# Token sums converted one step per second product, and three more PSUM banks in the first batch, in a fused sparse-attention and expert kernel

## The chip, the cores and the metric

The kernel runs on one core of a Trainium2 chip. The core has five engines with a queue each: PE (TensorE, matrix products, with its weight loads shown apart as PEld), DVE (VectorE), ACT (ScalarE), POOL (GpSimd) and SP (SyncE, which here only starts DMAs). An engine takes its instructions in the order of its queue, and one that waits holds up those behind it. The matrix results lie in PSUM, eight banks per partition. The metric is device time in microseconds, the median of three runs; the profile is one more execution with its own time.

## The reference

Two stages follow each other. The attention works on 4 batches, 8 heads, 768 tokens and 64 columns a head; a query block of 32 tokens sees its neighbours, the first and the last block, and three sampled blocks. The experts then take the attention's output `x` (3072 tokens by 512):

```
x = attention(q, k, v, sampled_blocks)         # 4 batches x 768 tokens, 512 columns
p = domain_probs / (sum(domain_probs) + 1e-9)
for e in range(4):
    h = max(x @ w1[e], 0)                      # 512 -> 1024
    out += p[:, e] * (h @ w2[e])               # 1024 -> 512
```

## The kernel before, in words

The first batch's attention runs alone, up to about 95 us. Then the experts of batch b run while the attention of batch b+1 is spread through them by `drive`. All five engines keep the order in which the program writes the instructions; no scheduler moves them.

The experts of a batch are cut into 8 chunks `c` (two for each expert, 512 hidden columns each). Inputs are kept as a high and a low part, so each product takes three matmuls for one. A step `first` makes one half product with `w1`: 6 matmuls of 128x384 (L537) into a PSUM bank. A step `second` makes 3 matmuls of 128x512 with `w2` (L595) into one of three banks `po`, and after four hidden tiles DVE adds the bank into `oacc` (L610).

Chunks 1 to 7 take seven products of sums of token blocks and of weight blocks for what would be eight plain ones; `ORDER` lists them. Chunk 0, the plain chunk, takes eight plain products of two steps each (`FIRST`, 16 steps), from the token blocks as they are: the operands `xo` 1, 2, 7 and 3. The first six products of chunk 0 follow each other on PE without a step `second` between them; this text calls them P0 to P5. They write the banks `v`, `w`, `v`, `w`, `v`, `w` (L551, `"vw"[i % 2]`, one buffer each). After the second step of a product, `finish` (L541) has ACT write the high part `hh` (L544) and then DVE the low part `hl` (L545); both read the bank, so the bank comes free when `hl` is written. `hl0` to `hl5` and `hh0` to `hh5` are those of P0 to P5.

The tokens' operands are made by the generator `conversion(b)` in 14 pieces, each one call of `convert`: a cast on ACT (`cast`, L399), the rest on DVE or POOL (`rest`, L402), or a difference of token blocks in place in `xr` on DVE (L417, L422, L425, L428). The plain chunk needs pieces 1 to 6. Pieces 7 to 12 make the sums of the seven products: piece 7 casts operand 5, piece 8 its rest and L422, piece 9 casts operand 6 and does L425, piece 10 its rest and L428, piece 11 casts operand 4, piece 12 its rest on POOL. Each of these reads what the one before it wrote. In the first batch 5 pieces are made ahead of the experts; in the others `convert(b + 1)` is called after every other `second` of the last batch's tail, up to 12 pieces (`PLAIN`), of which the tail has room for nine. What is left is called ahead of the steps of `first`, one piece per step.

The weights' operands `wo` come from ACT (L493) and POOL (L494), seven buffers; the eighth pair of a plain chunk is cut after P3, and P5's second step reads it.

Of the kernel before, what the change touches and what calls it, by code (L numbers as in the profile page):

```python
# [8 lines left out]
F32 = mybir.dt.float32  # L9
# [8 lines left out]
P = 128  # L18
# [5 lines left out]
def attention_moe_kernel(ctx: ExitStack, tc, qb, kb, vr, sampled, sampled_t, probs, w1, w2, out):  # L24
# [4 lines left out]
    NT, DM = out.shape  # L29
# [7 lines left out]
    HS = S // 2  # L37
# [25 lines left out]
    def f32(ap):  # L63
        return ap.bitcast(F32)
# [373 lines left out]
        xr.pop(b)  # L438
        yield

    EARLY, PLAIN = 3, 12
    pieces = {}
    steps = {}

    def convert(b, limit=PLAIN):
        if b in pieces and steps.get(b, 0) < limit:
            steps[b] = steps.get(b, 0) + 1
            next(pieces[b], None)
# [71 lines left out]
    W, pt, ut, zt = {}, {}, {}, {}  # L520
    po = {}

    def first(b, c, s, n):
        ps_m, cp, hp = later["m"], later["c"], later["h"]
        if c == 0:
            half, k, g = n
            w, x = wo[b, c, s, (half, k)], xo[XOF[k, g]]
            if g:
                wo.pop((b, c, s, (half, k)))
        else:  # L530
            w, x = wo.pop((b, c, s, n)), xo[n]

        def product(ps, fresh):
            m = 0
            for t in range(KH):
                for wi, xi in ((0, 0), (1, 0), (0, 1)):
                    nc.tensor.matmul(ps, w[:, wi, t], x[:, xi, t], start=fresh and m == 0,  # L537
                                     stop=m == 3 * KH - 1, skip_group_check=not fresh)
                    m += 1

        def finish(half, g, src):  # L541
            hh = hp.tile([P, HS], F32R, name=f"hh{g}", bufs=NH[g])
            hl = hp.tile([P, HS], F32R, name=f"hl{g}", bufs=NH[g])
            nc.scalar.activation(hh, src, AF.Relu)  # L544
            nc.vector.scalar_tensor_tensor(hl, src, 0.0, f32(hh), op0=ALU.max, op1=ALU.subtract)  # L545
            hs[c, 2 * s + half, g] = (hh, hl)

        if c == 0:
            i = [item for item, _ in FIRST].index((s, half, g))
            if k == 0:  # L550
                W[0] = ps_m.tile([P, HS], F32, name="vw"[i % 2], bufs=1)  # L551
            product(W[0], k == 0)
            if k == 1:
                finish(half, g, W.pop(0))
                for _ in range(FIRST[i][1]):
                    next(weights, None)
            return
        if n in (5, 2, 3):
            v = ps_m.tile([P, HS], F32, name="v", bufs=1)
            product(v, True)  # L560
        else:
            if n == 1:
                W[s] = ps_m.tile([P, HS], F32, name="w", bufs=1)
            product(W[s], n == 1)
        if n == 2:
            pt[s] = cp.tile([P, HS], F32, name="p1", bufs=1)
            nc.scalar.copy(pt[s], v)
        elif n == 1:
            nc.vector.tensor_add(pt[s], W[s], pt[s])  # L569
            finish(0, 0, pt[s])  # L570
        elif n == 5:
            zt[s] = cp.tile([P, HS], F32, name="z1", bufs=1)
            nc.scalar.copy(zt[s], v)
        elif n == 6:
            ut[s] = cp.tile([P, HS], F32, name="u1", bufs=1)
            nc.vector.tensor_add(ut[s], W[s], zt[s])
        elif n == 3:
            nc.vector.tensor_add(ut[s], v, ut[s])
            finish(0, 1, ut[s])
        elif n == 7:  # L580
            nc.vector.tensor_add(zt[s], W[s], zt[s])
            finish(1, 1, zt[s])
        else:
            finish(1, 0, W[s])
        next(weights, None)

    def second(b, c, g, f, j):
        e = c // CPE
        if f == 0:
            po[j] = later["m"].tile([P, DM], F32, name="po", bufs=HS // P)  # L590
        p = po[j]
        (hh, hl), (h2, l2) = hs[c, f, g], w2t[b, c, f]
        js = slice(j * P, (j + 1) * P)
        for n, (a, w) in enumerate(((hh, h2), (hh, l2), (hl, h2))):
            nc.tensor.matmul(p, a[:, js], w, start=f == 0 and n == 0,  # L595
                             stop=f == FT - 1 and n == 2)
        if j == HS // P - 1:
            hs.pop((c, f, g))
            if g == 0:
                w2t.pop((b, c, f))  # L600
                split_w2((b * NCH + c + 1) * FT + f)
        if f < FT - 1:
            return
        tok = b * KT + g * (HS // P) + j
        pe = pr[:, tok, e:e + 1]
        if c == 0:
            accs[tok] = later["o"].tile([P, DM], F32, name="oacc")
            nc.vector.tensor_scalar(accs[tok], p, pe, None, op0=ALU.mult)
        else:
            nc.vector.scalar_tensor_tensor(accs[tok], p, pe, accs[tok], op0=ALU.mult, op1=ALU.add)  # L610
        if c == NCH - 1:
            nc.sync.dma_start(out[tok * P:(tok + 1) * P, :], accs.pop(tok))
# [6 lines left out]
    def experts():  # L619

        L = len(ORDER)
        for b in range(B):
            one = [(0, s, (half, k, g)) for (s, half, g), _ in FIRST for k in range(2)]
            MORE = len(one) - L
            one += [(c, s, n) for c in range(1, NCH) for s, n in ORDER]
            two = [(c, g, f, j) for c in range(NCH) for g in (1, 0) for f in range(FT)
                   for j in range(HS // P)]
            p = q = 0
            after_first = False
            while q < len(two):  # L630

                wait = after_first and p < len(one) and one[p][2] == 4 and q < ready(p - MORE)
                if wait or p >= min(len(one), (q * NCH * L + (OFF + MORE) * len(two)) / len(two)):
                    second(b, *two[q])
                    q += 1
                    after_first = False
                    if p == len(one) and q % 2:
                        convert(b + 1)
                    yield T2, 2
                else:  # L640
                    if p < 2 * L:
                        convert(b, PLAIN if p <= L else PLAIN + 2)
                    first(b, *one[p])
                    p += 1
                    after_first = True
                    yield T1, 1

    def ready(p):

        return max(0, p - OFF + 1) * KT * FT // len(ORDER)  # L650

    stream = experts()
    done = [0.0]

# [169 lines left out]
```

## Time and profile before

| | |
|---|---|
| median of three runs | 1311.59 us (1309.81 to 1313.77) |
| the profiled execution's own time | 1304.3 us |
| its span | 1302.6 us |
| PE busy | 1252.1 us (96%) |
| DVE, ACT, POOL busy | 715.6, 622.6, 659.1 us (55%, 48%, 51%) |
| mean granted TensorE clock | 0.992 |

The profile gives each engine's busy time, the waits with what released them, the instructions in order of time, and by stretch the granted clock as a share of full speed (2.4 GHz). "Idle before" is the time in which the engine had nothing running ahead of that instruction; the releaser named is the event that came last. A PE row's duration runs past the start of the next row, since matmuls are pipelined; the pace is read from one start to the next.

### The profile page before, as it was taken

To read this page: it belongs to the slowest core of one execution; us is meant where nothing else is said; L and a number is where in the kernel's file an instruction comes from. 1 tells how busy PE (TensorE), PEld (TensorE's weight loads), DVE (VectorE), ACT (ScalarE), POOL (GpSimd) and SP (SyncE) were. 2 spreads that over 40 slices of the span, in tenths; PEclk is the share of its full clock that TensorE was granted. 3 is DMA by queue.
4 is the path that set the end of the run, shared out by engine and by line. 5 is a ranking of instruction groups with operands and counts; after the bars stand their busy time and mean duration, and the time that the engine had idled before them with its cause. 6 is when DMAs were issued, how large, how long until landed. Compare 5 with 4: busy or idle time off the path is not lost.

```text
span 1302.6 us, 31439 instructions
## 1 busy us (share of the span) xinstructions
PE 1252.1 (96%) x12286; PEld 1080.3 (83%) x12286; DVE 715.6 (55%) x1690; ACT 622.6 (48%) x1642; POOL 659.1 (51%) x848
## 2 busy tenths in 40 slices
PE   7678999999998999999999899999999999999998
PEld 4557888888887888888888878888888888888887
DVE  5555655655555555655554555556555545555553
ACT  4673445555543445555554344455554434444441
POOL 5543545566445346654545454566553635454551
PEclk9989999999999999999999999999999999999999
DMA  8843334353325124443425231443441322222211
GB/s 257 240 137 113 91 98 124 113 155 103 98 81 191 49 82 118 136 128 99 145 66 174 97 90 34 139 139 123 123 123 37 105 74 65 65 65 66 65 49 57
DMA packets 60048, 140.49 MB, mean 108 GB/s; under 512 B 7163, under 2 KB 8700, under 8 KB 59900
## 3 DMA queue, kind: packets, MB, share of 16 engines
q1 hardware_dynamic: 52816, 115.41, 28.3%
q0 software_dynamic: 7040, 23.07, 6.4%
q8 instruction: 96, 1.57, 0.5%
q14 instruction: 52, 0.43, 0.1%
q10 hardware_dynamic: 44, 0.00, 0.0%
HBM read 132.17 MB, written 6.29 MB: 106 GB/s over the span
## 4 chain that ended last, share of the span: by engine, by line
PE 90%; DVE 6%; issue 2%; ACT 2%; DVEq 0%; DMA 0%; ACTq 0%
PE po L595 40%; PE w L537 20%; PE v L537 15%; PE o L291 4%; PE tp L278 3%; PE s L256 2%; PE s L251 2%; PE sw L325 1%; DVE oacc L610 1%; DVE xo L402 1%; PE ow L356 1%; PE x L310 1%; DVE hl L545 1%; PE tw L346 1%; DVE xr L422 1%
## 5 line engine op out<-in xcount | busy, mean ns | idle before, releaser
L494 POOL TENSOR_TENSOR wo<-r,wo 128x256 fp32r<-128x256 f32 x368 | 288.8, 788 | 412.0 <-ACT wo L493 411.1
L595 PE MATMUL po<-h,hh 128*128 128x512 f32 x768 | 311.4, 405 | 3.7 <-DVE oacc L610 2.1
L537 PE MATMUL w<-xo,wo 128*128 128x384 f32 x1536 | 310.8, 339 | 1.3 <-DVE hl L545 1.3
L595 PE MATMUL po<-h,hl 128*128 128x512 f32 x768 | 303.9, 396 | 0.0
L595 PE MATMUL po<-l,hh 128*128 128x512 f32 x768 | 303.7, 395 | 0.0
L537 PEld LDWEIGHTS w<-xo,wo 128*128 128x128 f32 x1536 | 275.1, 189 | 22.2 <-DVE hl L545 1.7
L537 PE MATMUL v<-xo,wo 128*128 128x384 f32 x1200 | 244.3, 341 | 13.3 <-DVE hl L545 12.2
L537 PEld LDWEIGHTS v<-xo,wo 128*128 128x128 f32 x1200 | 217.3, 190 | 31.5 <-DVE hl L545 13.8
L493 ACT CAST wo<-r 128x256 fp32r<-128x256 f32 x368 | 146.7, 401 | 157.1 <-DVE r L487 97.7
L510 POOL TENSOR_TENSOR l<-r,h 128x512 fp32r<-128x512 f32 x128 | 171.2, 1338 | 41.9 <-ACT h L509 41.6
L595 PEld LDWEIGHTS po<-h,hl 128*128 128x128 f32 x768 | 144.4, 188 | 33.4
L595 PEld LDWEIGHTS po<-h,hh 128*128 128x128 f32 x768 | 144.3, 188 | 27.2 <-DVE oacc L610 4.7
L595 PEld LDWEIGHTS po<-l,hh 128*128 128x128 f32 x768 | 144.6, 188 | 14.0
L610 DVE SCALAR_TENSOR_TENSOR oacc<-po,pr,oacc 128x512 f32<-128x512 f32 x168 | 121.5, 745 | 15.3 <-PE po L595 14.5
L569 DVE TENSOR_TENSOR p<-w,p 128x384 f32<-128x384 f32 x56 | 31.2, 558 | 161.6 <-PE w L537 161.6
L269 ACT ACTIVATE p<-p,mx 128x256 f32<-128x256 f32 (+1 forms) x192 | 95.4, 498 | 45.5 <-DVE mx L266 45.5
L136 POOL DMA_INDIRECT v<-in_vr_dram,vidx x88 | 86.0, 977 | 45.0 <-issue 16.1
L509 ACT CAST h<-r 128x512 fp32r<-128x512 f32 x128 | 79.4, 621 | 27.2 <-PE po L595 24.8
L494 POOL TENSOR_TENSOR wo<-s,wo 128x256 fp32r<-128x256 f32 x56 | 41.2, 736 | 97.5 <-ACT wo L493 97.5
L266 DVE CUSTOM_DVE_ANT_1 p<-s,mask 128x256 f32<-128x256 f32 (+1 forms) x192 | 69.8, 418 | 35.3 <-PE s L256 35.0
L545 DVE SCALAR_TENSOR_TENSOR hl<-w,hh 128x384 fp32r<-128x384 f32 x72 | 40.1, 557 | 75.4 <-ACT hh L544 75.4
L544 ACT ACTIVATE hh<-p 128x384 fp32r<-128x384 f32 x56 | 29.4, 525 | 91.7 <-DVE p L569 91.7
(115 smaller groups left out, 1406.7 us busy)
## 6 DMA issues: line engine op xcount, KB each, us to landing
r<-in_w_dram SPq DMA_DIRECT2D x64, 512.0 KB, 4.1
r<-in_w_dram SPq DMA_DIRECT2D x128, 256.0 KB, 2.6
v<-in_vr_dram SPq DMA_DIRECT2D x44, 384.0 KB, 4.8
k<-in_kb_dram SPq DMA_DIRECT2D x8, 768.0 KB, 6.7
out_dram<-oacc SPq DMA_DIRECT2D x24, 256.0 KB, 2.7
v<-in_vr_dram SPq DMA_DIRECT2D x44, 128.0 KB, 5.1
q<-in_qb_dram SPq DMA_DIRECT2D x20, 256.0 KB, 5.4
v<-in_vr_dram SPq DMA_DIRECT2D x4, 1024.0 KB, 8.0
```

The source lines that it names most:

```text
L136: nc.gpsimd.indirect_dma_start(out=v[:, i, 1], out_offset=None, in_=vr, element_offset=b * S * DM, in_offset=bass.IndirectOffsetOnAxis(ap= ...
L266: nc.vector.tensor_tensor_reduce(p.rearrange("p (a b) -> p a b", b=BLOCK), s[h][:n, i], mk, -SCALE, 3.0e38, ALU.add, ALU.min, mx[:n])
L269: nc.scalar.activation(p, p, AF.Exp, bias=mx[:n], scale=-1.0, accum_out=self.sums[:n, m:m + 1])
L291: nc.tensor.matmul(o[cs, m], self.pt[:, 2 * m + k, cs], vs[c][:, k, e], start=k == 0, stop=k == 1)
L493: nc.scalar.copy(o[:, 0], src)
L494: nc.gpsimd.tensor_sub(o[:, 1], src, f32(o[:, 0]))
L509: nc.scalar.copy(h, r)
L510: nc.gpsimd.tensor_sub(l, r, f32(h))
L537: nc.tensor.matmul(ps, w[:, wi, t], x[:, xi, t], start=fresh and m == 0, stop=m == 3 * KH - 1, skip_group_check=not fresh)
L545: nc.vector.scalar_tensor_tensor(hl, src, 0.0, f32(hh), op0=ALU.max, op1=ALU.subtract)
L595: nc.tensor.matmul(p, a[:, js], w, start=f == 0 and n == 0, stop=f == FT - 1 and n == 2)
L610: nc.vector.scalar_tensor_tensor(accs[tok], p, pe, accs[tok], op0=ALU.mult, op1=ALU.add)
```

## The change

Three edits. In the tail of a batch the next batch's conversion stops at 6 pieces (`NEEDED`) and not at 12. In `first`'s loop, a piece is called only ahead of the second step of a product (odd `p`) while the plain chunk lasts, and not ahead of every step. In the first batch alone P2, P3 and P4 write the first 384 columns of the three `po` banks, which no `second` has used yet, and not `v`, `w`, `v`.

```diff
-    EARLY, PLAIN = 3, 12
+    EARLY, NEEDED, PLAIN = 3, 6, 12
...
             if k == 0:
-                W[0] = ps_m.tile([P, HS], F32, name="vw"[i % 2], bufs=1)
+                if b == 0 and 2 <= i < 5:
+
+                    W[0] = ps_m.tile([P, DM], F32, name="po", bufs=HS // P)[:, :HS]
+                else:
+                    W[0] = ps_m.tile([P, HS], F32, name="vw"[i % 2], bufs=1)
...
                     if p == len(one) and q % 2:
-                        convert(b + 1)
+                        convert(b + 1, NEEDED)
                     yield T2, 2
                 else:
-                    if p < 2 * L:
-                        convert(b, PLAIN if p <= L else PLAIN + 2)
+
+                    if p % 2 or p >= L + MORE:
+                        convert(b, PLAIN if p < L else PLAIN + 2)
                     first(b, *one[p])
```

The first place is ACT's queue at the border from batch 0 to batch 1, from the last casts of the tail (`h` is a part of `w2`) to hh3. Before:

```order
L509 CAST h_6477<-r_6290 128x512
L399 CAST xo_6486<-xr 128x768
L509 CAST h_6494<-r_6334 128x512
L399 CAST xo_6512<-xr 128x768
L509 CAST h_6518<-r_6461 128x512
L399 CAST xo_6535<-xr 128x768
L544 ACTIVATE hh_6543<-v 128x384
L544 ACTIVATE hh_6561<-w 128x384
L544 ACTIVATE hh_6578<-v 128x384
L544 ACTIVATE hh_6595<-w 128x384
```

The three rows `xo` are the casts of operands 5, 6 and 4, all ahead of hh0. After the change, with the same stretch up to hh4:

```order
L509 CAST h_6477<-r_6290 128x512
L509 CAST h_6492<-r_6334 128x512
L509 CAST h_6511<-r_6461 128x512
L399 CAST xo_6526<-xr 128x768
L544 ACTIVATE hh_6534<-v 128x384
L544 ACTIVATE hh_6553<-w 128x384
L399 CAST xo_6564<-xr 128x768
L544 ACTIVATE hh_6573<-v 128x384
L544 ACTIVATE hh_6592<-w 128x384
L493 CAST wo<-r_6246 128x256
L493 CAST wo<-r_6352 128x256
L399 CAST xo_6611<-xr 128x768
```

Only the cast of operand 5 still stands ahead of hh0; that of 6 stands behind hh1, that of 4 behind hh3.

The second place is DVE's queue at the same border, from the differences L417 to hl3. Before:

```order
L417 TENSOR_TENSOR xr<-xr 128x2x384
L402 TENSOR_TENSOR xo_6486<-xr,xo_6486 128x768
L422 TENSOR_TENSOR xr<-xr 128x2x384
L610 SCALAR_TENSOR_TENSOR oacc<-po,pr,oacc 128x512 x2
L425 TENSOR_TENSOR xr<-xr 128x2x384
L610 SCALAR_TENSOR_TENSOR oacc<-po,pr,oacc 128x512
L402 TENSOR_TENSOR xo_6512<-xr,xo_6512 128x768
L428 TENSOR_TENSOR xr<-xr 128x2x384
L545 SCALAR_TENSOR_TENSOR hl_6544<-v,hh_6543 128x384
L545 SCALAR_TENSOR_TENSOR hl_6562<-w,hh_6561 128x384
L545 SCALAR_TENSOR_TENSOR hl_6579<-v,hh_6578 128x384
L545 SCALAR_TENSOR_TENSOR hl_6596<-w,hh_6595 128x384
```

All rests and differences of the sums stand ahead of hl0. After the change (L614 is the L610 of before):

```order
L417 TENSOR_TENSOR xr<-xr 128x2x384
L614 SCALAR_TENSOR_TENSOR oacc<-po,pr,oacc 128x512 x3
L545 SCALAR_TENSOR_TENSOR hl_6535<-v,hh_6534 128x384
L402 TENSOR_TENSOR xo_6526<-xr,xo_6526 128x768
L422 TENSOR_TENSOR xr<-xr 128x2x384
L545 SCALAR_TENSOR_TENSOR hl_6554<-w,hh_6553 128x384
L425 TENSOR_TENSOR xr<-xr 128x2x384
L545 SCALAR_TENSOR_TENSOR hl_6574<-v,hh_6573 128x384
L402 TENSOR_TENSOR xo_6564<-xr,xo_6564 128x768
L428 TENSOR_TENSOR xr<-xr 128x2x384
L545 SCALAR_TENSOR_TENSOR hl_6593<-w,hh_6592 128x384
```

The five rows stand between hl0 and hl3 now: two behind hl0, one behind hl1, two behind hl2.

## Rows read from the trace of the kernel before

**Rows 1.** The page: busy time by engine, and the costliest groups.
```profile
PE 1252.1 (96%) x12286; PEld 1080.3 (83%) x12286; DVE 715.6 (55%) x1690; ACT 622.6 (48%) x1642; POOL 659.1 (51%) x848
...
L494 POOL TENSOR_TENSOR wo<-r,wo 128x256 fp32r<-128x256 f32 x368 | 288.8, 788 | 412.0 <-ACT wo L493 411.1
```

**Rows 2.** Waits of PE: us in total, times, longest us.
```profile
PE v L537 <- DVE hl L545: 12.2, 5, 3.1
...
PE po L595 <- DVE oacc L610: 2.1, 6, 0.4
...
PE w L537 <- DVE hl L545: 1.3, 1, 1.3
```

**Rows 3.** PE in order of time, first batch: start, us, instruction, idle before.
```profile
96.35 2.37 PE L537 MATMUL v<-xo,wo 128*128 128x384 f32 x12 [1.12 <-DVE xr L312]
98.57 2.25 PE L537 MATMUL w<-xo,wo 128*128 128x384 f32 x12
102.58 2.36 PE L537 MATMUL v<-xo,wo 128*128 128x384 f32 x12 [1.77 <-DVE hl L545]
...
114.16 0.40 PE L595 MATMUL po<-h,hh 128*128 128x512 f32 x1
```

**Rows 4.** PE in order of time, border from batch 0 to 1.
```profile
411.15 2.27 PE L537 MATMUL v<-xo,wo 128*128 128x384 f32 x12
413.26 2.25 PE L537 MATMUL w<-xo,wo 128*128 128x384 f32 x12
418.56 3.17 PE L537 MATMUL v<-xo,wo 128*128 128x384 f32 x12 [3.05 <-DVE hl L545]
...
424.40 2.24 PE L537 MATMUL v<-xo,wo 128*128 128x384 f32 x12
426.48 2.27 PE L537 MATMUL w<-xo,wo 128*128 128x384 f32 x12
428.59 0.39 PE L595 MATMUL po<-h,hh 128*128 128x512 f32 x1
```

**Rows 5.** By stretch: us, busy (count) PE, PEld, DVE, ACT, POOL; clock, DMA share, GB/s.
```profile
96.35:114.16 17.81, 13.47 (x73) 12.51 (x74) 11.41 (x13) 6.98 (x13) 5.85 (x5) 1.00 0.60 221
418.56:424.40 5.84, 5.84 (x24) 5.84 (x25) 0.96 (x2) 0.49 (x1) 0.86 (x1) 0.71 0.01 4
1047.64:1053.47 5.83, 5.83 (x24) 5.83 (x25) 0.97 (x2) 0.49 (x1) 0.86 (x1) 0.71 0.00 0
```

**Rows 6.** ACT in order of time, first batch and border from batch 0 to 1.
```profile
100.72 0.83 ACT L399 CAST xo<-xr 128x768 fp32r<-128x768 f32 x1 [2.81 <-DVE xr L417]
...
416.69 0.83 ACT L399 CAST xo<-xr 128x768 fp32r<-128x768 f32 x1 [3.67 <-DVE xr L428]
417.43 0.48 ACT L544 ACTIVATE hh<-v 128x384 fp32r<-128x384 f32 x1
...
421.77 0.49 ACT L544 ACTIVATE hh<-v 128x384 fp32r<-128x384 f32 x1 [3.48 <-PE v L537]
```

**Rows 7.** DVE in order of time, border from batch 0 to 1.
```profile
409.71 1.93 DVE L422 TENSOR_TENSOR xr<-xr 128x768 f32<-128x768 f32 x1
...
414.41 1.38 DVE L402 TENSOR_TENSOR xo<-xr,xo 128x768 fp32r<-128x768 f32 x1
415.71 0.94 DVE L428 TENSOR_TENSOR xr<-xr 128x768 f32<-128x768 f32 x1
417.94 0.56 DVE L545 SCALAR_TENSOR_TENSOR hl<-v,hh 128x384 fp32r<-128x384 f32 x1 [1.29 <-ACT hh L544]
...
422.29 0.56 DVE L545 SCALAR_TENSOR_TENSOR hl<-v,hh 128x384 fp32r<-128x384 f32 x1 [3.32 <-ACT hh L544]
```

**Rows 8.** DVE, then POOL: a difference beside work of POOL.
```profile
98.08 2.60 DVE L417 TENSOR_TENSOR xr<-xr 128x768 f32<-128x768 f32 x1
...
97.98 1.89 POOL L402 TENSOR_TENSOR xo<-xr,xo 128x768 fp32r<-128x768 f32 x1 [2.68 <-ACT xo L399]
408.82 3.98 POOL L510 TENSOR_TENSOR l<-r,h 128x512 fp32r<-128x512 f32 x2
```

## The prediction

> **What bounds the kernel now.** The page's first part shows PE busy for 1252.1 us of a span of 1302.6, the three other engines for about half [rows 1]. So only what PE waits for, or what slows PE, can move the time, and the next view is PE's waits [rows 2]. In the experts' part its largest entry is the `w1` products waiting for DVE's `hl`: 12.2 us in 5 waits with results in bank `v`, 1.3 us in one in bank `w`. The order of time then tells where. In the first batch P0 starts at 96.35 and P1 at 98.57; P2 only at 102.58, after 1.77 us of idleness, and the first `second` at 114.16 [rows 3]. At the border from batch 0 to 1, P0 starts at 411.15, P1 at 413.26, P2 only at 418.56 after 3.05 us, P4 at 424.40, P5 at 426.48, and the first `second` at 428.59 [rows 4]. The last view is the stretch table, for the clock: in the first batch's stretch it stayed at 1.00 in spite of the waits; in the two products after a border's wait it was 0.71, which is time at both levels, 1.2 and 2.4 GHz, and this stands the same at all three borders (the first and the last are shown) [rows 5].
>
> **Why P2 waits.** P2 wants bank `v` back from P0, so it wants hl0. At the border ACT stands in the cast of operand 4 until 417.43, because that cast waited 3.67 us for DVE's L428; only then hh0 begins, and hl0 at 417.94 [rows 6, 7]. P0 had ended some 4 us earlier. The work in the way is pieces 8 to 11. In the first batch it is piece 7, whose cast waited 2.81 us for L417 [rows 6].
>
> **What PE's stretch would take without waits.** Borders: P0 to P1 takes 413.26 - 411.15 = 2.11 us, P4 to P5 2.08, P5 to the first `second` 2.11 [rows 4]. With 2.08 for the others the six products take 2.11 + 4 x 2.08 + 2.11 = 12.54 us, where they took 428.59 - 411.15 = 17.44. The excess is 4.90: 5.84 - 2 x 2.08 = 1.68 of it is the low clock in P2 and P3 [rows 5], the rest the wait and the restart behind it. First batch: 2.22 + 4 x 2.08 + 2.11 = 12.65 against 17.81, an excess of 5.16 [rows 3].
>
> **First edit: pieces by the second step, 6 in the tail.** It removes no work. The pieces stand in ACT's and DVE's queues behind the `hl` for which PE waits. I follow one border with the times of before. DVE's two instructions of a piece cost 0.95 each (L428: 0.94) [rows 7]. A bank comes free, with nothing in the way, 1.31 us after its product: for the product that the next one follows at 424.40 - 2.87 = 421.53, hh began at 421.77 and hl ended at 422.29 + 0.56 = 422.85 [rows 6, 7]; it is needed 2.08 after, so 0.77 are to spare.
>
> P0 would end at 413.26, hl0 at 414.6; P2 wants it at 415.34: no wait. Piece 8 then holds DVE for 1.9 us, to 416.45; hl1 could have begun at 416.1 and begins 0.35 late; it ends at 417.0, and P3 wants it at 417.42. Piece 9's cast (0.83) follows hh1 on ACT and waits for piece 8 to 416.45, so it ends at 417.3, before P2 does at 417.42: hh2 isn't late. L425 ends at 417.95, before hl2 begins at 418.2; P4 wants hl2 at 419.50 and has it at 418.75. Piece 10 holds DVE to 420.6, hl3 ends at 421.15, P5 wants it at 421.58. So each wait goes with 0.4 us or more to spare. Gain: 3 x 4.90 = 14.7 us, the low clock with it, since no idleness is left ahead of P2.
>
> **Second edit: three banks in the first batch.** P2, P3 and P4 write banks that nobody has used, so they wait for no `hl`; P5 wants `w` from hl1, four products old. This cover is needed: L417 ends at 98.08 + 2.60 = 100.68 [rows 8], hl0 behind it at 101.25, where P2 would want `v` at 100.65. It adds a wait: the first `second` steps want the `po` banks back from hl2 to hl4. By the same queue hl2 ends near 105, hl3 near 106.5, hl4 near 109, and the third bank is asked for only after P5 and some 4 us of mixed steps, past 112. That costs nothing; with each `hl` later by a difference as slow as L417 (1.65 over 0.95) still nothing. Gain: 5.16 us.
>
> **What is late next.** The eighth weight pair is cut after P3 and read in P5's second step, 2.08 + 1.04 = 3.12 us later. ACT and POOL need about 0.24 for the handoff, 0.48 for hh3, under 0.5 for the cast and 0.79 on POOL [rows 1], together 2.0; POOL's rest of operand 4 stood ahead of it and now stands behind. It holds with 1.1 to spare. Operands 4, 5 and 6 are read first by chunk 1's products, ten and more microseconds after their new places. DMAs keep their places in the queue. Behind that only PE itself remains, and 2.1 us of short waits for `oacc` [rows 2], which I leave as they are.
>
> **The sum.** 5.16 + 14.7 = 19.9 us. The profiled execution's own time of 1304.3 becomes 1284.4. The runs' median lies 7.3 above that execution; I carry the saving over unchanged: 1311.59 - 19.9 = 1291.7.
>
> **The cost that the trace does not show** is that of the moved DVE instructions in their new place. Some rows show them slow: L402 took 1.38, L422 1.93, L417 2.60, the last two beside work of POOL, which ran from 408.82 to 412.80 and from 97.98 to 99.87 [rows 7, 8]. From below a piece's instruction costs 0.95 (not less: no row is shorter), from above 2.60. I take 0.95, because in the new places POOL's `l` work should be over and its weight work not begun: L428, at 415.71 in the same stretch of a border, took 0.94 [rows 7]. With 2.60 for one of the two in each pair, hl1 and hl3 come 1.65 late, 0.4 is spare, so P3 and P5 wait 1.2 each: 2 x 3 x 1.2 = 7.2 lost.
>
> The Trainium skill speaks against me here: SBUF — State Buffer, section Who interferes with whom, says that a VectorE instruction with two SBUF inputs and a GpSimd instruction that reads SBUF take turns on one shared port, the one that came second standing still for the whole of the other. L417, begun 0.10 after POOL's 1.89, agrees with it: it lost 1.65 [rows 8]. L422 beside POOL's pair lost 0.98, less than the rule gives, and POOL was slowed too. By the rule the sum holds as long as POOL is idle in the new places, and is the 7.2 smaller if it is not.
>
> **Rivals.**
> A, the moved pairs meet POOL. Waits of about 1.2 us at P3 and P5 of each border stay: 1291.7 + 7.2 = 1298.9. For it: POOL's weight cuts after P3 begin near 420.5, as piece 10 ends. Against it: POOL's last `l` should end before piece 8.
> B, the low clock at a border is not of the wait's making and stays: 1291.7 + 3 x 1.68 = 1296.7. For it: all three borders show 0.71. Against it: P0 and P1 there ran at the full pace, and the low stretch begins at the wait's end.
> C, the change does not do what it says at the borders: another queue holds hh0 back as long. Only the first batch gains: 1311.6 - 5.2 = 1306.4. For it: a cast still stands ahead of hh0. Against it: that is operand 5's, whose input L417 is done with the tail.
> D, slower. The pieces now close a ring between two `hl` of the same bank: hl0, L402, L422, the cast on ACT, hh2, hl2. Two products give 4.16 us; the ring takes 0.95 + 0.95 + 0.83 + 0.48 + 0.56 = 3.77, so it decides once its two DVE instructions take over 0.39 more. With L417's 2.60 for both it takes 7.07, 2.91 over, near the 3.05 after which the clock fell; then each of the border's two rings costs 2.91 + 1.68 = 4.59, the border 9.2 where 4.9 went. 1311.6 - 5.2 + 3 x 4.3 = 1319.3. For it: 0.39 is little. Against it: POOL would have to stand beside all four instructions. The skill's port rule above is its cause if it comes.
>
> **How the numbers follow.** Forecast 0.74, A 0.13, B 0.03, C 0.03, D 0.04; 0.03 for part of D, where losses and gains cancel. About 0.3%, 3.9 us, is what a measurement of this kernel can tell. The forecast, A, B and C are faster by more: 0.93. The cancelling case is the same: 0.03. D is slower: 0.04. The range goes from 1291.7 less the 2.2 us by which a run lay off the median and the 2.1 of `oacc` waits that may shrink as the tail's DVE work does, 1287.4, to A with 1 us of that spread, 1300: it holds the forecast, A and B.
>
> **What would show it.** PE's waits: the entries for `hl` gone or under 1 us in total. First batch: P0 to the first `second` in about 12.7 us. Each border: 12.5, at a clock of 1.00, with hh0 within 0.4 us of P0's end. DVE's L422 and L428 between `hl` at 0.95. Wrong if P3 or P5 waits at the borders (A), if a clock under 1 stays without a wait (B), if P2 still waits for hl0 (C), or if a new wait for weights or for `po` stands in the first batch.

## The result, and the profile after

The changed kernel takes 1292.69 us (four runs, 1292.29 to 1293.01) where the kernel before takes 1312.06 (four runs): a ratio of 0.9858, 95% interval 0.9846 to 0.9870, 19.4 us less. The prediction said 1291.7 and 19.9 less.

PE's waits of the changed kernel (us in total, times, longest us), the rows that answer to [rows 2]:

```profile
PE po L599 <- DVE oacc L614: 3.3, 6, 1.0
PE po L599 <- DVE oacc L612: 1.5, 3, 0.6
PE v L537 <- DVE xr L312: 1.1, 1, 1.1
```

No row for `hl` is left: the 13.5 us of before are gone. What remains in the experts' part is the short waits for `oacc`. Their total, 4.8 us here, is 1.0 more than in the kernel before; two later traces of the changed kernel have 3.8 again, as before.

PE in order of time at the border from batch 0 to 1, to be read against [rows 4]:

```profile
413.93 2.27 PE L537 MATMUL v<-xo,wo 128*128 128x384 f32 x12
416.03 2.24 PE L537 MATMUL w<-xo,wo 128*128 128x384 f32 x12
418.11 2.24 PE L537 MATMUL v<-xo,wo 128*128 128x384 f32 x12
420.19 2.24 PE L537 MATMUL w<-xo,wo 128*128 128x384 f32 x12
422.27 2.24 PE L537 MATMUL v<-xo,wo 128*128 128x384 f32 x12
...
426.46 0.39 PE L599 MATMUL po<-h,hh 128*128 128x512 f32 x1
```

Each product starts 2.08 to 2.10 after the one before it, and the six take 12.53 us where they took 17.44. The other two borders take 12.54 each.

DVE at the same border, in the new order, to be read against [rows 7]:

```profile
416.76 0.56 DVE L545 SCALAR_TENSOR_TENSOR hl<-v,hh 128x384 fp32r<-128x384 f32 x1 [1.88 <-ACT hh L544]
417.23 0.95 DVE L402 TENSOR_TENSOR xo<-xr,xo 128x768 fp32r<-128x768 f32 x1
418.21 0.96 DVE L422 TENSOR_TENSOR xr<-xr 128x768 f32<-128x768 f32 x1
419.09 0.55 DVE L545 SCALAR_TENSOR_TENSOR hl<-w,hh 128x384 fp32r<-128x384 f32 x1
419.56 0.95 DVE L425 TENSOR_TENSOR xr<-xr 128x768 f32<-128x768 f32 x1
420.92 0.56 DVE L545 SCALAR_TENSOR_TENSOR hl<-v,hh 128x384 fp32r<-128x384 f32 x1 [0.41 <-ACT hh L544]
421.39 0.95 DVE L402 TENSOR_TENSOR xo<-xr,xo 128x768 fp32r<-128x768 f32 x1
422.25 0.95 DVE L428 TENSOR_TENSOR xr<-xr 128x768 f32<-128x768 f32 x1
423.12 0.55 DVE L545 SCALAR_TENSOR_TENSOR hl<-w,hh 128x384 fp32r<-128x384 f32 x1
```

The moved instructions take 0.95 or 0.96, L422 half of its 1.93 of before. hl1 ends at 419.64 and P3 starts at 420.19; hl3 ends at 423.67 and P5 starts at 424.35. So 0.55 and 0.68 us are to spare, and hl1 and hl3 are the two without idle time ahead of them: there DVE sets the pace. POOL's weight cuts (the instructions at L494 that make the low parts of the weights) begin just behind L428's end at 423.20:

```profile
423.33 1.44 POOL L494 TENSOR_TENSOR wo<-r,wo 128x256 fp32r<-128x256 f32 x2 [7.18 <-ACT wo L493]
```

The first batch in the changed kernel, on PE, against [rows 3]:

```profile
102.10 3.92 PE L537 MATMUL v<-xo,wo 128*128 128x384 f32 x12 [1.12 <-DVE xr L312]
105.86 2.24 PE L537 MATMUL w<-xo,wo 128*128 128x384 f32 x12
107.94 6.40 PE L537 MATMUL po<-xo,wo 128*128 128x384 f32 x36
114.18 2.27 PE L537 MATMUL w<-xo,wo 128*128 128x384 f32 x12
116.28 0.39 PE L599 MATMUL po<-h,hh 128*128 128x512 f32 x1
```

And the stretch table for P0 there, and for P2 and P3 at the border (columns as in [rows 5]):

```profile
102.10:105.86 3.76, 3.76 (x12) 3.76 (x13) 2.92 (x2) 1.54 (x2) 1.87 (x1) 0.55 0.98 358
...
418.11:422.27 4.16, 4.16 (x26) 4.16 (x25) 3.72 (x7) 1.82 (x3) 0.00 (x0) 1.00 0.39 129
```

The border runs at 1.00 now. In the first batch the waits are gone too, but P0 itself ran near the lower of the two levels and took 3.76 us to P1's start, not 2.22; so the stretch takes 14.18 us, not the 12.65 that I had.

The two profiled executions differ by less than the medians: spans of 1302.6 and 1291.1, 11.5 us. P0 begins at 96.35 in the one and at 102.10 in the other, 5.75 us of attention ahead of all that the change touches. Whether the change has a part in that is one of the questions below.

### The profile page after: what moved, and what is told of

It reads as the page before. It is cut to its first block, busy times and chain, and to the rows that moved or that the text cites. A ratio compares the mean times of both kernels' runs of the same rounds, so it can differ in the third digit from the quotient of the medians.

```text
span 1291.1 us, 31439 instructions
## 1 busy us (share of the span) xinstructions
PE 1253.1 (97%) x12286; PEld 1080.2 (84%) x12286; DVE 712.7 (55%) x1690; ACT 623.8 (48%) x1642; POOL 653.3 (51%) x848
## 4 chain that ended last, share of the span: by engine, by line
PE 94%; DVE 3%; issue 2%; ACT 1%; DMA 0%; DVEq 0%; ACTq 0%
PE po L599 41%; PE w L537 21%; PE v L537 16%; PE o L291 4%; PE tp L278 3%; PE s L256 2%; PE s L251 2%; PE sw L325 2%; PE ow L356 1%; PE tw L346 1%; DVE oacc L614 1%; PE x L310 1%; DVE hl L545 1%; PE po L537 0%; ACT p L269 0%
## 5 line engine op out<-in xcount | busy, mean ns | idle before, releaser
L494 POOL TENSOR_TENSOR wo<-r,wo 128x256 fp32r<-128x256 f32 x368 | 288.9, 789 | 410.9 <-ACT wo L493 410.0
L537 PE MATMUL w<-xo,wo 128*128 128x384 f32 x1524 | 307.2, 338 | 0.0
L537 PEld LDWEIGHTS w<-xo,wo 128*128 128x128 f32 x1524 | 271.3, 188 | 20.9 <-DVE z L585 0.5
L537 PE MATMUL v<-xo,wo 128*128 128x384 f32 x1176 | 237.1, 338 | 1.1 <-DVE xr L312 1.1
L537 PEld LDWEIGHTS v<-xo,wo 128*128 128x128 f32 x1176 | 211.7, 189 | 17.8 <-DVE xr L312 1.3
L510 POOL TENSOR_TENSOR l<-r,h 128x512 fp32r<-128x512 f32 x128 | 165.1, 1291 | 43.2 <-ACT h L509 42.9
L614 DVE SCALAR_TENSOR_TENSOR oacc<-po,pr,oacc 128x512 f32<-128x512 f32 x168 | 121.6, 745 | 28.0 <-PE po L599 27.2
L494 POOL TENSOR_TENSOR wo<-s,wo 128x256 fp32r<-128x256 f32 x56 | 41.3, 737 | 99.5 <-ACT wo L493 97.8
```

Source lines behind the costliest of these rows:

```text
L494: nc.gpsimd.tensor_sub(o[:, 1], src, f32(o[:, 0]))
L510: nc.gpsimd.tensor_sub(l, r, f32(h))
```

## The experiments

The ratios are to the kernel before on the same chip, with 95% intervals. The first four ran together on a chip where the kernel before took 1306.54 us, the next four on one where it took 1311.95.

**The tail's limit alone.**

```diff
-    EARLY, PLAIN = 3, 12
+    EARLY, NEEDED, PLAIN = 3, 6, 12
...
-                        convert(b + 1)
+                        convert(b + 1, NEEDED)
```

> The tail's limit of 6 pieces alone; a piece ahead of every step and the banks of before. Theory (a bank comes free when hl has got through DVE's queue): at a border hl0 is in time (about 0.2 us to spare), but L425, L402 and L428 now stand ahead of hl1, so the wait moves from P2 to P3 and shrinks from 3.05 to about 0.9 us; without a long wait the clock stays 1.00, so a border takes 12.5 + 1.0 = 13.6 us and 3 x 3.9 = 11.6 us are saved; the first batch's stretch stays at 17.8. Ratio to before 0.991. Rival (the low clock belongs to the border, not to the wait): 0.71 stays, the border takes 15.2, ratio 0.995. Rival (the tail's pieces are the whole cause): no wait at P3 either, ratio 0.989.

Ratio 0.9907 (0.9890 to 0.9924). PE at a border (the other two alike), and the rest of operand 5 on DVE:

```profile
415.54 2.38 PE L537 MATMUL v<-xo,wo 128*128 128x384 f32 x12 [0.24 <-DVE hl L545]
418.61 2.35 PE L537 MATMUL w<-xo,wo 128*128 128x384 f32 x12 [0.69 <-DVE hl L545]
...
412.61 1.42 DVE L402 TENSOR_TENSOR xo<-xr,xo 128x768 fp32r<-128x768 f32 x1 [0.68 <-ACT xo L399]
```

A border takes 14.0 us, not 13.6: the wait moved to P3 as expected, and P2 kept 0.24, since L402, which met POOL's `l` (411.92 to 413.21), took 1.42 instead of the 0.95 I had reckoned. The clock stayed at full pace (P4 follows P3 by 2.18, then P5 by 2.08), so the low clock does not belong to the border. The first stretch, from P0 to the first `second`, stands at 17.79, with P0 slow (3.71 to P1's start, where the kernel before has 2.22) and a wait at P2 that has shrunk to 0.22:

```profile
102.33 2.37 PE L537 MATMUL v<-xo,wo 128*128 128x384 f32 x12 [0.22 <-DVE hl L545]
```

**The step edit alone.**

```diff
-                    if p < 2 * L:
-                        convert(b, PLAIN if p <= L else PLAIN + 2)
+                    if p % 2 or p >= L + MORE:
+                        convert(b, PLAIN if p < L else PLAIN + 2)
```

> A piece ahead of each second step alone; the tail makes nine pieces and the banks are those of before. Theory: at a border L402 and L428 of piece 10 still stand ahead of hl0, the cast of operand 4 no longer ahead of hh0, so hl0 ends near 417.2 and not 418.5 on the clock of before: P2 waits about 1.8 us and not 3.05. First batch: P2 waits about 0.6 us for hl0 behind L417, P3 and P4 for nothing: 4.5 of the 5.2 us go. If the clock falls only after the long wait, a border takes 14.5, saved 4.5 + 3 x 2.9 = 13 us, ratio 0.990; if 1.8 us of idleness are enough, 16.2, saved 4.5 + 3 x 1.2 = 8 us, ratio 0.994. Rival (the edit does nothing without the tail's limit): only the first batch gains, ratio 0.9965.

Ratio 0.9896 (0.9879 to 0.9912). A border, and the clock of the two products after the wait:

```profile
415.27 2.35 PE L537 MATMUL v<-xo,wo 128*128 128x384 f32 x12 [1.68 <-DVE hl L545]
```
```profile
415.27:419.54 4.27, 4.27 (x25) 4.27 (x26) 1.11 (x2) 1.22 (x3) 1.84 (x1) 1.00 0.24 89
```

1.68 us of idleness left the clock at 1.00, and a border takes 14.48 us, as the first case said. In the first batch no product from P1 to P5 waits, without the new banks; the wait of 0.6 that I expected at P2 did not come. The stretch takes 14.19, P0 again slow (3.75 to P1's start). P1 and P2:

```profile
101.78 2.25 PE L537 MATMUL w<-xo,wo 128*128 128x384 f32 x12
103.87 2.24 PE L537 MATMUL v<-xo,wo 128*128 128x384 f32 x12
```

**The three banks alone.**

```diff
-                W[0] = ps_m.tile([P, HS], F32, name="vw"[i % 2], bufs=1)
+                if b == 0 and 2 <= i < 5:
+                    W[0] = ps_m.tile([P, DM], F32, name="po", bufs=HS // P)[:, :HS]
+                else:
+                    W[0] = ps_m.tile([P, HS], F32, name="vw"[i % 2], bufs=1)
```

> The three banks of the first batch alone. Theory: P2, P3 and P4 wait for nothing and P5 not for hl1, but the eighth weight pair is now late, since hh3 stands behind the casts on ACT and POOL's rest of operand 4 ahead of the pair: P5's second step waits 1 to 2 us. The first stretch takes 14 to 14.5 us and not 17.8, the borders keep 17.4 at 0.71: saved 3.5 us, ratio 0.997. Rival (the banks are worth their whole 5.2 us alone): ratio 0.996, the stretch 12.7. The trace tells these apart, the times do not.

Ratio 0.9985 (0.9975 to 0.9994). PE at P5's second step in the first batch:

```profile
109.52 0.44 PE L537 MATMUL w<-xo,wo 128*128 128x384 f32 x1 [0.54 <-ACT wo L493]
111.05 1.14 PE L537 MATMUL w<-xo,wo 128*128 128x384 f32 x5 [1.08 <-POOL wo L494]
```

The eighth weight pair became the new wait, as expected: 0.54 for its high part and 1.08 for its low part. The stretch takes 16.1 us and not 14 to 14.5, and the ratio is not the 0.997 that I expected. Of the 3.4 us over my 12.65, P5 with its two waits is 2.15; the other 1.29, which I had not counted, is P0's low clock (3.51 to P1's start). One border happened to lose more to the clock (18.67), the others stand at 17.43.

**The changed kernel without the banks, twice, and itself again.**

```diff
-                if b == 0 and 2 <= i < 5:
-                    W[0] = ps_m.tile([P, DM], F32, name="po", bufs=HS // P)[:, :HS]
-                else:
-                    W[0] = ps_m.tile([P, HS], F32, name="vw"[i % 2], bufs=1)
+                W[0] = ps_m.tile([P, HS], F32, name="vw"[i % 2], bufs=1)
```

> The changed kernel without the three banks: both edits of the conversion stay. Theory: borders as in the changed kernel, 12.5 us at 1.00; in the first batch P2 alone waits for hl0, which stands behind the slow L417, about 0.6 us, so the stretch takes 13.3 us at full clock. 0.6 us over the changed kernel, ratio to before 0.986, not to be told from it. Rival (the first batch's gain comes from the banks): P2, P3 and P4 wait, the stretch takes near 17, ratio 0.989.

Ratio 0.9844 (0.9828 to 0.9861), against 0.9858 for the whole change on another chip. No product from P1 to P5 of the first batch waits; the stretch takes 13.94 with P0 at 3.50. Since the ratio suggested that the banks cost time, both ran side by side:

> The changed kernel itself, beside the same without the three banks on one chip. Theory: P0 runs at the low clock in both, as in five of the six profiles so far, and P2 then asks for bank v some 1.5 us later than the prediction had it, after hl0 is written; so the banks are worth 0 to 0.6 us and the two medians lie within 1 us of each other. Rival (the banks cost time, as the ratios 0.9858 and 0.9844 from two chips would have it): this one is 1.5 to 2 us the slower.

> The changed kernel without the three banks, once more, for the comparison named with the changed kernel's run: median within 1 us of it by the theory, 1.5 to 2 us below it by the rival. In the trace no wait for hl in the first batch if P0 runs at the low clock, one of about 0.6 us at P2 if it runs at the full one.

1294.24 and 1293.93 us, ratios 0.9849 (0.9831 to 0.9867) and 0.9858 (0.9843 to 0.9873); the first stretches take 14.18 and 14.19. The banks are worth nothing that can be measured here, and cost nothing; P0 ran at the low clock in both.

**Longer work between two `hl`.**

```diff
-        rest(5, b11, nc.vector)
+        for _ in range(3):
+            rest(5, b11, nc.vector)
...
-        rest(6, b11, nc.vector)
+        for _ in range(3):
+            rest(6, b11, nc.vector)
```

> The changed kernel with DVE's rests of operands 5 and 6 written three times over (the same values). DVE's work between hl0 and hl1 and between hl2 and hl3 grows by 1.8 us each, and nothing else changes. Theory (DVE's queue between two hl sets the wait; 0.55 us are to spare at P3 and 0.68 at P5 by the changed kernel's trace): P3 waits 1.2 to 1.3 us, P5 1.5, no fall of the clock; a border takes 12.5 + 3.1 = 15.6, the run 9 us more than the changed kernel, ratio to before 0.992 to 0.993. Rival (the margins are larger than read, the rests hidden): ratio as the changed kernel's, 0.985.

Ratio 0.9949 (0.9934 to 0.9964), 11.2 us over the changed kernel. PE at a border, then DVE's L428 (L430 in this kernel) and POOL beside it:

```profile
424.07 2.35 PE L539 MATMUL w<-xo,wo 128*128 128x384 f32 x12 [1.32 <-DVE hl L547]
...
430.17 2.35 PE L539 MATMUL w<-xo,wo 128*128 128x384 f32 x12 [1.67 <-DVE hl L547]
```
```profile
428.16 1.49 DVE L430 TENSOR_TENSOR xr<-xr 128x768 f32<-128x768 f32 x1
...
427.31 2.92 POOL L496 TENSOR_TENSOR wo<-r,wo 128x256 fp32r<-128x256 f32 x2 [8.74 <-ACT wo L495]
```

The waits are 1.32 and 1.67, about those expected; a border takes 16.03 and not 15.6, 3.5 us over the changed kernel's, three of them 10.5. Pushed late enough to meet POOL's weight cuts, L428 took 1.49 and not 0.95: the encounter of rival A, which the changed kernel misses by 0.12 or 0.13 us at each of its borders. In the first batch 1.2 us of waits for `hl` came besides, which I had not counted; so the run is 11.2 us over the changed kernel, not 9.

With `range(5)` in place of `range(3)`:

> The same with the two rests five times over: 3.6 us more DVE work in each of the two places. Theory: P3 waits 3.1 us, near the 3.05 after which the clock fell at the borders before, so P3 and P4 run at a clock of about 0.7 and lose 1.7 to 2.9 us; P5 waits 1.5 to 2; a border takes 19 to 20, the run some 20 to 23 us more than the changed kernel, ratio to before 1.001 to 1.004: the prediction's rival D brought about by hand. Rival (a wait alone does not lower the clock): 5 to 8 us less than that, ratio 0.996 to 0.998.

Ratio 1.0110 (1.0094 to 1.0126), slower than the kernel before. PE's two waits at a border, and the clock after each:

```profile
429.16 3.48 PE L539 MATMUL w<-xo,wo 128*128 128x384 f32 x12 [3.31 <-DVE hl L547]
437.66 2.36 PE L539 MATMUL w<-xo,wo 128*128 128x384 f32 x12 [2.50 <-DVE hl L547]
```
```profile
429.16:432.43 3.27, 3.27 (x12) 3.27 (x13) 3.20 (x5) 0.74 (x2) 0.00 (x0) 0.63 0.03 5
...
437.66:439.86 2.20, 2.20 (x13) 2.20 (x13) 1.40 (x3) 1.03 (x3) 0.73 (x1) 1.00 0.01 2
```

After 3.31 us of idleness P3 ran at 0.63; after 2.50 us P5 ran at 1.00. A border takes 20.45 us, 7.9 over the changed kernel's, where I had 6.5 to 7.5; P5's wait was the larger part of the miss. The first batch lost 4.8 us to waits for the weight pair and for `hl`, which I had not counted. In sum the miss was 10 us: 32 and not 20 to 23 over the changed kernel, of which the profiled execution of this kernel shows 27, the borders' 24 and the better part of the first batch's waits; what its other runs, 3 to 7 us longer, lost besides, no trace shows.

**Both kernels for one more trace on one chip.**

> The kernel before, for one more trace of it. The profiled execution of before lay 7.3 us under its median, that of the changed kernel on its median, and P0 began at 96.35 in the one and at 102.10 in the other. Theory (the stretch ahead of P0 varies from run to run and chip to chip, whatever the kernel): P0 begins within 1 us of where it begins in the changed kernel's run on the same chip, and the three borders stand again at 17.4 us with 3.05 of idleness. If P0 runs at the low clock, P2 waits some 0.2 us only and the first stretch is still 17.8, because hl0 is held up by DVE and not by P0. Rival (the change makes the attention ahead of P0 slower): P0 begins 5 us or more earlier than in the changed kernel.

> The changed kernel for one more trace on the same chip as the kernel before. Theory: P0 begins where it begins in the other, within 1 us; the first stretch takes 14.2 us with P0 at the low clock or 12.7 at the full one; the borders 12.5. So the two spans differ by 17 to 19 us, and not by 11.5 as the first two profiles do. Rival: P0 begins 5 us later or more, and the spans differ by 11 to 12.

The first P0 in the kernel before, then in the changed one:

```profile
106.23 2.35 PE L537 MATMUL v<-xo,wo 128*128 128x384 f32 x12 [1.12 <-DVE xr L312]
```
```profile
106.65 3.33 PE L537 MATMUL v<-xo,wo 128*128 128x384 f32 x12 [1.12 <-DVE xr L312]
```

P0 begins 0.42 us apart, and the spans are 1313.5 and 1294.5, 19.0 apart. So the 5.75 us between the first two profiles were not the change's. In the ten traces of the experiments P0's begin goes with the chip, whatever the edit: 96 to 98 on the first chip, 102 to 105 on the second, 106 to 107 on this one. The chip of the first two profiles is not on record.

## Why the prediction was right, point by point

**The border term** (4.90 each, 14.7 in all) came out to the tenth: 17.44 became 12.53 and 12.54. The hl waits and the low clock went together, as the step on P2 to P5 had it. The two edits of the conversion share the term and don't add: the tail's limit alone takes a border to 14.0, the steps alone to 14.48, both to 12.53. Either alone leaves a difference ahead of an `hl` that is asked for.

**The margins** for P3 and P5 were 0.42 and 0.43 in the working, 0.55 and 0.68 in the trace; the two products named as the tight ones are those that waited when DVE's work was made longer by 2 us in each place.

**The first-batch term** was mis-sized, and its edit misnamed. I had 5.16 us, for P0 at the full clock, and put it under the second edit. The changed kernel's stretch is 14.18 to 14.22 in three traces, so 3.6 of the 17.8 went. P0 ran at the low clock, for most of its time at least, in all ten traces of edited kernels (3.13 to 3.76 us to P1's start, not 2.22; where it was 3.13, P1 was slow too, with 2.74 to P2's start), and at the full one in both of the kernel before. Up to P0 the engines' queues are the same in all of them, and PE's 1.12 us of idleness ahead of P0 too, so I leave open why. In the kernel before it would have cost nothing, as the tail's limit alone shows, since the wait behind it shrinks by as much (0.22 instead of 1.77, stretch 17.79). And the gain is the step edit's: it has 14.19 without the banks. The step that failed is the one that called this cover needed: with P0 slow, P2 asks for bank `v` some 1.5 us later, after hl0 (in steps_only, without the banks, P2 follows P1 at once). With P0 at the full clock the banks should save the 0.6 us that the prediction's times give; no run of that kind came up, so it stays open.

**What is late next** was read rightly for the changed kernel. The banks alone show what the order was worth: with the casts still ahead of it on ACT and the rest of operand 4 on POOL, the weight pair made P5 wait 1.6 us.

**The rivals.** B fell with the border at 1.00, and with 1.68 us of idleness that left the clock alone. C fell with the traces. A did not occur at the borders, but it was close: 0.12 or 0.13 us between L428 and POOL. In the first batch of the changed kernel it did occur: POOL's cuts come beside L402 and L428, which take 1.42 and 1.49 there. It cost PE nothing, because these two stand behind hl3 in that batch, and hl4, which they hold up, is not asked for early. So an encounter costs a moved instruction 0.47 to 0.54 in these places, not the 1.65 that I priced it at. The prediction took L422's loss of 0.98 for less than a full wait behind POOL, and that was a misreading: when L422 began, at 409.71, POOL's first `l` (408.82 to 410.82) had only 1.11 us left. D did not occur either, but its mechanism is real: with about 4 us of added work between two `hl`, put there by hand and not by POOL, a border costs 7.9 us more than in the changed kernel, where 4.9 had been gained, and the kernel is slower than before. Of the two falls of the clock that D counted in a border, one came.

**The sum.** The traces account for 14.7 + 3.6 = 18.3, and the medians say 19.4 with an interval of 17.1 to 20.2. That 19.4 lies so near the predicted 19.9 is in part luck, since the first-batch term of that sum was 1.5 too large. Against the sum stands about 1 us that the first trace of the changed kernel lost in waits for `oacc` (3.3 against 2.1). The measurement does not tell 18.3 and 19.9 apart: both lie inside the interval.

## What to carry to other kernels

When an engine of high use waits for a buffer, read which instruction stood in the releasing engine's queue ahead of the release, and ask whether it had to be there: here the work was needed ten microseconds later, and no wait of PE came of moving it behind the release. A wait of a few microseconds on PE costs more than itself when the clock falls behind it: here a wait of 1.68 us made a border 1.95 longer, and one of 3.05, with the low clock behind it, 4.90. And two edits aimed at one wait should each be run alone: the banks looked like 5 us by the trace of before and were worth nothing measurable once the order was mended.

## What the runs showed of the hardware

At the borders a low clock followed every wait of 3.05 to 3.31 us ahead of a product, twelve in all (three borders each of the kernel before, twice, of the banks alone and of rests_x5). It followed none of the waits of 0.2 to 2.50 there (steps_only, tail_only, rests_x3, and P5 in rests_x5). The length of the last wait is not the whole of it: P0 of the first batch ran slow in ten of twelve traces and at the full clock in two, with the same 1.12 us of idleness right ahead of it each time. What decides there is not settled. What the fall costs varies too: borders of the kernel before took 17.2 to 18.7 us.

DVE and POOL hold each other up, and which of them loses goes by which began second. In tail_only POOL's `l` took 1.29, about what it takes alone (1.28 at 414.87 in the changed kernel), and L402, begun with 0.60 of it left, lost 0.47. Where the two engines find each other at work in turn, both lose. In the first batch of the changed kernel the three cuts of POOL took 0.74, 1.46 and 1.45, where one alone takes 0.74, beside a slow L402 and a slow L428 on DVE:

```profile
113.29 1.42 DVE L402 TENSOR_TENSOR xo<-xr,xo 128x768 fp32r<-128x768 f32 x1
114.63 1.49 DVE L428 TENSOR_TENSOR xr<-xr 128x768 f32<-128x768 f32 x1
...
113.16 3.56 POOL L494 TENSOR_TENSOR wo<-r,wo 128x256 fp32r<-128x256 f32 x3 [7.57 <-ACT wo L493]
```

The Trainium skill, SBUF — State Buffer, section Who interferes with whom, has the second one blocked for the whole of the first's instruction; these rows agree with it, instruction by instruction: each that began second lost about what the other's had left.

The length of an `hl` varies with it. The `hl` that read a PSUM bank (`v`, `w`, `po`) took at most 0.56 us in all twelve traces. All that took over 0.6, 28 to 31 in each trace, read sums that had been put into SBUF (`p`, `u`, `z`), and each of them stood beside work of POOL. One in the middle of the first batch took 2.21 in the changed kernel's first trace, where two instructions of POOL followed each other without a turn for DVE:

```profile
272.04 2.21 DVE L545 SCALAR_TENSOR_TENSOR hl<-p,hh 128x384 fp32r<-128x384 f32 x1 [0.59 <-issue]
...
271.82 1.31 POOL L510 TENSOR_TENSOR l<-r,h 128x512 fp32r<-128x512 f32 x1
273.07 0.75 POOL L494 TENSOR_TENSOR wo<-r,wo 128x256 fp32r<-128x256 f32 x1
```

It took 1.58 in the kernel before and 1.60 in the changed kernel's third trace, where POOL's second instruction was the slow one (1.12 and 1.14). The wait for `oacc` behind it was 1.04 in the first and 0.41 and 0.43 in the others. Why POOL kept the turn in the one trace stays open.
